# A gated attention block on one Trainium2 core: one more feature group by seven products, and one subtraction of the output pairs placed later

## The chip, the cores and the metric

The kernel runs on one core of one Trainium2 chip. The metric is the device time of one execution in microseconds (us); smaller is better. The kernel before takes 742.05 us, the median of 3 runs between 741.96 and 743.94.

## What is computed

```python
xn = layernorm(x)                                        # x: 2048 tokens x 640
q, k, v = split(xn @ wqkv)                               # 32 heads of 20
logits[s, w] = (q[s] . k[s - 2w]) * 20**-0.5             # w = 0..7; positions before the start are masked
s = (sum_w softmax(logits)[s, w] * v[s - 2w]) @ wo
g = silu(((xn @ w_gate) * (xn @ w_up)) @ w_down)         # 1536 features between
return x + s * g
```

All of it is fp32. TensorE multiplies in fp32r, so each operand is split into a high part (rounded to fp32r) and a low part (the rest), and each product is made of three: high by high, high by low, low by high (`ALL3`).

## The kernel before

The 2048 tokens are four chunks of 512, and the 1536 features are twelve feature groups of 128 (`f` = 0 to 11). `split` (L112) is the helper for the parts: ScalarE (ACT) copies the high part (L114), and the engine that is passed in subtracts it (L115), GpSimd (POOL) for nearly all weights.

**Two ways to make a feature group.** The straight way, `gate_up(f, ch)` (L636), is 15 matmuls of 512 columns for the gate and 15 for the up product of one chunk. The other way, `group(f, c0)` (L1296), makes gate and up of one feature group for two chunks together by Strassen's scheme (in its variant with seven products): seven products in the order j = 0, 5, 2, 1, 4, 3, 6, here called n0 to n6, with 6, 9, 6, 9, 6, 9 and 9 matmuls of 512 columns, 54 in place of 60. It needs sums of weight blocks (`w_add`: S1, S2, S3, d5, S4, all on POOL, L1281) and their high and low parts (`w_split`: G, S, R, U). The seven products pile up in three PSUM banks: A (tile name g), C (u) and B (q). After n0, n2, n3 and n4 ACT copies the bank out (`hold`, L1304) before a later product adds to it: n2 goes on A, which `hold` of n0 must have read, and n5 goes on C, which `hold` of n3 must have read. VectorE (DVE) and POOL put the copies together (L1307, L1310, L1313, L1317, L1320); L1310 and L1313 run on DVE for a group of chunks 2 and 3 with `f >= VEC`, else on POOL. L1320 releases bank A.

**Order of the work.** TensorE (PE) works through one list written out by hand. After a start with `f` = 0 and 1 and the first query/key/value blocks (`qkv`, L425) come `gate_up(1, 2)`, `gate_up(0, 3)`, `gate_up(1, 3)` (from L1169), then the `qkv` blocks of m = 1 to 4 (L1397 on), then a loop over f = 2 to 10 with `group(f, 2)` and `group(f, 0, 1)`, then `group(11)`, four straight products of `f` = 11 (L1363, L1372), ten tokens' worth of output pairs (`pair_product`, L1030), the rest of the output projection, and the down products (`product`, L895). In the loop, `two_places` puts the preparation of the weights of `f + 1` behind given products of the two groups: sums behind n5 and n6 of the first and n0 and n1 of the second, parts behind n2, n4, n5 and n6 of the second.

**Beside it.** The attention is a generator (L467) that `advance` lets go on by a credit after each piece of PE work; it is emitted in order, twelve units, each of DVE products and sums (L536, L543, L504), additions on POOL (L510), and one softmax with the exponent on ACT (L565) between two DVE steps (L563 and L570). Each engine works through its own queue in order, so what is emitted between two instructions sets what stands between them.

**Loads of weights.** `load_wf(f)` (L178, the transfer L180) brings 640 KB for one feature group into one of two buffers named wraw, which the sums of `w_add` share; the next load waits until the last reader of its buffer on POOL is done. The transfers are issued by SyncE (SP), which also has one queue in order.

**Output pairs.** For ten token tiles in pairs the output projection is made by seven products as well (`pair_product(p, j)`). `hi_pair` and `lo_pair` (L1021, DVE) make the parts of the next pair. After j = 0 to 2 ACT copies the bank into one buffer `o` (L1045); DVE adds from it at L1051, L1048 and L1053 (j = 5), and the next pair's first copy (L1045) must wait until L1053 has read the buffer. PE's next product on that bank waits for the copy.

## Time and profile before

| | |
|---|---|
| median of 3 runs | 742.05 us |
| profiled execution | 742.42 us |
| its span, first to last instruction | 740.0 us |
| mean granted TensorE clock | 0.999 |
| PE busy | 732.1 us, 99% |
| DVE busy | 625.0 us, 84% |
| POOL busy | 454.3 us, 61% |
| ACT busy | 302.5 us, 41% |

A line of the timeline has the start, the time, the engine, the line of the kernel, the operation, the tile written and the tiles read, the shape, and in square brackets how long the engine stood idle before it and on what. PEld is the load of PE's weights, which runs beside its matmuls. A line of the waits has the waiting instruction, what it waited for, the sum, the count and the longest. A line of the windows has the stretch, its length, and the busy time of PE, PEld, DVE, ACT and POOL. A line of the chain has start, duration and what it was; x15 is fifteen matmuls. A line of the groups has the count, the busy time, the mean in ns, and the idle time before.

### The profile page before, as it was taken

How to read it: one execution, taken by the hardware profiler on the slowest of the kernel's cores; microseconds unless marked ns; L12 is line 12 of the kernel's file. 1: busy time of each engine (PE TensorE's matmuls, PEld its weight loads, DVE VectorE, ACT ScalarE, POOL GpSimd, SP SyncE). 2: the span in 40 equal slices, each digit the busy share in tenths (PEclk: the TensorE clock that was granted, in tenths of full speed). 3: DMA queues.
4: the chain of work that ended last, by engine and by line, in shares of the span. 5: the costliest groups of instructions: out<-in, count | busy, mean ns of one | idle time of the engine just before them, and what ended most of it. 6: DMA issues, size and time to landing. Idle time of an engine off the chain costs nothing.

```text
span 740.0 us, 11087 instructions
## 1 busy us (share of the span) xinstructions
PE 732.1 (99%) x4048; PEld 667.8 (90%) x4048; DVE 625.0 (84%) x728; ACT 302.5 (41%) x578; POOL 454.3 (61%) x384
## 2 busy tenths in 40 slices
PE   8999999999999999999999999999999999999997
PEld 6989989988999998888888887888999999999997
DVE  7676998799787989899989999978998777777775
ACT  5668312423332333233233332335556664444442
POOL 6159919887688889798879979577559700000000
PEclk9999999999999999999999999999999999999999
DMA  9465582767364649452634443269558655555534
GB/s 325 166 203 173 216 276 88 241 220 241 93 183 144 232 152 362 119 186 60 205 100 127 153 128 101 83 180 243 149 160 235 223 208 193 192 193 192 193 107 142
DMA packets 103491, 132.96 MB, mean 180 GB/s; under 512 B 22696, under 2 KB 74404, under 8 KB 103438
## 3 DMA queue, kind: packets, MB, share of 16 engines
q1 hardware_dynamic: 86286, 114.25, 48.9%
q10 hardware_dynamic: 16000, 12.78, 5.3%
q0 software_dynamic: 1152, 5.24, 2.2%
q8 instruction: 31, 0.51, 0.3%
q14 instruction: 22, 0.18, 0.1%
HBM read 83.58 MB, written 47.81 MB: 178 GB/s over the span
## 4 chain that ended last, share of the span: by engine, by line
PE 94%; DMA 2%; DVE 1%; POOL 1%; issue 1%; ACT 1%; SPq 0%; ACTq 0%; DVEq 0%; POOLq 0%
PE g L1335 15%; PE q L433 10%; PE u L1335 10%; PE q L905 9%; PE u L433 8%; PE g L433 8%; PE u L905 6%; PE q L1335 5%; PE g L124 5%; PE u L124 5%; PE g L905 3%; PE e L905 3%; PE q L124 2%; PE e L433 1%; PE e L124 1%; PE q L1042 1%
## 5 line engine op out<-in xcount | busy, mean ns | idle before, releaser
L510 POOL TENSOR_TENSOR o<-o,t 128x960 f32<-128x960 f32 (+1 forms) x66 | 133.2, 2019 | 10.2 <-DVE t L504 9.4
L504 DVE TENSOR_TENSOR t<-e,kv 128x960 f32<-128x960 f32 (+1 forms) x96 | 99.6, 1038 | 16.4 <-POOL o L510 16.4
L536 DVE TENSOR_TENSOR t<-q,kv 128x1920 f32<-128x1920 f32 (+1 forms) x48 | 92.4, 1926 | 4.3 <-ACT s L447 2.9
L543 DVE TENSOR_REDUCE lg<-t 128x96 f32<-128x1920 f32 (+1 forms) x48 | 92.3, 1922 | 0.2
L433 PE MATMUL q<-s,xc 128*128 128x360 f32 (+1 forms) x450 | 83.1, 334 | 0.1
L115 POOL TENSOR_TENSOR s<-wraw,s 128x384 fp32r<-128x384 f32 (+6 forms) x57 | 69.6, 1235 | 19.3 <-ACT s L114 19.2
L1304 ACT ACTIVATE gh<-g 128x512 f32<-128x512 f32 x57 | 34.1, 599 | 113.5 <-PE g L1335 109.7
L433 PEld LDWEIGHTS q<-s,xc 128*128 128x128 f32 x450 | 74.9, 188 | 4.4 <-POOL s L115 0.6
L433 PE MATMUL u<-s,xc 128*128 128x360 f32 (+1 forms) x360 | 65.7, 334 | 0.0
L433 PEld LDWEIGHTS u<-s,xc 128*128 128x128 f32 x360 | 60.2, 188 | 2.3
L433 PE MATMUL g<-s,xc 128*128 128x360 f32 (+1 forms) x330 | 61.5, 337 | 0.0
L1335 PE MATMUL u<-xc,s 128*128 128x512 f32 x228 | 58.1, 390 | 0.0
L433 PEld LDWEIGHTS g<-s,xc 128*128 128x128 f32 x330 | 55.7, 188 | 2.6
L1335 PE MATMUL g<-s,s 128*128 128x512 f32 x228 | 57.9, 389 | 0.0
L905 PE MATMUL q<-xc,s 128*128 128x320 f32 x342 | 55.5, 309 | 0.0
L905 PEld LDWEIGHTS q<-xc,s 128*128 128x128 f32 x342 | 51.5, 188 | 0.0
L1335 PEld LDWEIGHTS u<-xc,s 128*128 128x128 f32 x228 | 42.8, 188 | 9.3 <-POOL s L115 0.4
L1335 PEld LDWEIGHTS g<-s,s 128*128 128x128 f32 x228 | 42.8, 188 | 8.8
L114 ACT ACTIVATE s<-wraw 128x384 fp32r<-128x384 f32 (+6 forms) x58 | 32.6, 581 | 29.8 <-PE g L1335 10.2
L1335 PE MATMUL g<-xc,s 128*128 128x512 f32 x171 | 42.0, 390 | 0.2 <-ACT gh L1304 0.2
L1335 PE MATMUL q<-xc,pk 128*128 128x512 f32 x171 | 41.8, 389 | 0.0
L510 POOL TENSOR_TENSOR o<-t 128x960 f32<-128x960 f32 (+1 forms) x11 | 22.1, 2011 | 28.9 <-DVE t L504 27.1
(364 smaller groups left out, 1563.6 us busy)
## 6 DMA issues: line engine op xcount, KB each, us to landing
h_scr<-gh SPq DMA_DIRECT2D x48, 256.0 KB, 2.6
wraw<-in_wgu SPq DMA_DIRECT2D x11, 640.0 KB, 4.6
kv<-qkv_scr SPq DMA_DIRECT2D x14, 480.0 KB, 5.7
t<-h_scr SPq DMA_DIRECT2D x8, 768.0 KB, 7.3
qkv_scr<-s ACTq DMA_DIRECT2D x17, 360.0 KB, 3.5
kv<-qkv_scr SPq DMA_DIRECT2D x14, 367.5 KB, 6.8
s_scr<-gh SPq DMA_DIRECT2D x16, 320.0 KB, 4.1
gh<-s_scr SPq DMA_DIRECT2D x16, 320.0 KB, 3.7
```

Source lines behind the costliest of these rows:

```text
L114: nc.scalar.activation(hi, raw, AF.Copy)
L115: eng.tensor_sub(lo, raw, hi.bitcast(F32))
L124: nc.tensor.matmul(acc, a, b, start=first and n == 0, stop=last and n == len(runs) - 1)
L433: nc.tensor.matmul(p, xT[(r * NE + i) // TPC][a][:, k, t0:t0 + P], wq[m][b][k], start=n == 0, stop=n == len(runs) - 1, skip_group_check=ac ...
L504: nc.vector.tensor_mul(t.rearrange("p (n d) -> p n d", d=DH), e[:, :, w].unsqueeze(2).to_broadcast([P, NE * nh, DH]), v)
L510: return NE * c * cost, lambda: eng.tensor_add(y, z, t)
L536: nc.vector.tensor_mul(t, q, k)
L543: nc.vector.tensor_reduce(out=lg[:, :, j:j + 2].rearrange("p n a -> p a n"), in_=t.rearrange("p a (n d) -> p a n d", d=DH), op=ALU.add, ax ...
L905: nc.tensor.matmul(p, y[:, i, k], wd_t[name][k][:, l], start=new and r == 0, stop=r == len(runs) - 1, skip_group_check=True)
L1042: nc.tensor.matmul(b, y, w, start=new and r == 0, stop=r == len(runs) - 1, skip_group_check=True)
L1304: nc.scalar.activation(kept[j], b["ACACABA"[j]], AF.Copy)
L1335: nc.tensor.matmul(y, w, x, start=j in (0, 1, 5) and r == 0, stop=r == len(runs) - 1, skip_group_check=True)
```

## The change

`gate_up(1, 2)` and `gate_up(1, 3)` go; feature group 1 of chunks 2 and 3 is made by `group(1, 2)` after the `qkv` blocks and ahead of `group(2, 2)`. Its weights, which the start has already loaded and split in another form for chunks 0 and 1, are loaded again. All that was prepared for `f` = 2 during the `qkv` blocks is now prepared for `f` = 1, and the weights of `f` = 2 are prepared within `group(1, 2)` itself, behind n2 to n6. `VEC` is 1, so that L1310 and L1313 of the new group are on DVE. Apart from that, `lo_pair(p + 1, 1)` goes behind `pair_product(p, 5)`.

```diff
-VEC = 2
+VEC = 1
     split_wq(1, nc.gpsimd)
-    gate_up(1, 2)
     gate_up(0, 3)
-    gate_up(1, 3)
-    F_TWO = 2
+    F_TWO = 1
     def first_parts():
         for name in ("S1", "S2", "S3", "d5", "S4"):
-            w_add(2, name)
+            w_add(1, name)
             yield
-        w_split(2, "S")
+        w_split(1, "S")
             if (m, r, i) == (last - 1, 1, 6):
-                load_wf(2)
+                load_wf(1)
             elif m == last and n == NT - 3:
-                w_split(2, "G")
+                w_split(1, "G")
     step(100)
-    w_split(2, "R")
-    w_sum.pop(2)
-    load_wf(3)
+    w_split(1, "R")
+    w_sum.pop(1)
+    load_wf(2)
-    for f in range(2, f1):
+    for f in range(1, f1):
         places.clear()
+        if f == 1:
+            places.update({(0, 2): splits("G"), (0, 3): sums("S1", "S2"), (0, 4): sums("S3", "d5", "S4"),
+                           (0, 5): splits("S"), (0, 6): splits("R", "U")})
+            group(1, 2)
+            continue
         places.update(two_places)
-        if f == F_TWO:
+        if f == 2:
             for n in range(3):
                 places[0, n] = lambda f, n=n: load_late(n)
         group(f, 2)
@@
         wd_splits()
         if more:
             lo_pair(p + 1, 2)
+        pair_product(p, 5)
+        if more:
             lo_pair(p + 1, 1)
-        pair_product(p, 5)
```

The diff moves the lines of `group` up by two: `hold` is L1304 before and L1302 after, `w_add`'s sum L1281 and L1279, the copies' additions L1307 to L1320 are L1305 to L1318.

**ACT at the first group.** The rows from the last parts of the weights ahead of the first group to its third and fourth `hold`. Before, where the first group is `group(2, 2)` (its banks are g_2641 and u_2642):

```order
L114 ACTIVATE s_2636<-wraw_2292 128x384
L114 ACTIVATE s_2636<-wraw_2226 128x384
L1304 ACTIVATE gh_2651<-g_2641 128x512
L565 ACTIVATE e_70<-lg_2449 128x256
L494 ACTIVATE q_2_69<-q_2543 128x640
L1304 ACTIVATE gh_2682<-g_2641 128x512
L1304 ACTIVATE gh_2696<-u_2642 128x512
```

Of the change, where it is `group(1, 2)` (g_2542 and u_2543); wraw_2540 is the weights of `f` = 2, wraw_2594 their sums:

```order
L114 ACTIVATE s_2537<-wraw_2190 128x384
L114 ACTIVATE s_2537<-wraw_2129 128x384
L1302 ACTIVATE gh_2552<-g_2542 128x512
L1302 ACTIVATE gh_2572<-g_2542 128x512
L114 ACTIVATE pk_2488<-wraw_2540 128x640
L1302 ACTIVATE gh_2592<-u_2543 128x512
L1302 ACTIVATE gh_2606<-g_2542 128x512
L114 ACTIVATE s_2353<-wraw_2594 128x768
L114 ACTIVATE s_2537<-wraw_2594 128x384
L114 ACTIVATE s_2537<-wraw_2540 128x384
L1302 ACTIVATE gh_2650<-g_2642 128x512
```

The high part of G of `f` = 2 now stands between the second and the third `hold` of the group, and three more high parts stand ahead of the first `hold` of the next group.

**POOL at the same place**, of the change: from the low part of G of `f` = 1 (wraw_2129) to that of U of `f` = 2. The third row from the top is an addition of the attention; the fourth is the low part of R of `f` = 1, the last reader of the buffer into which `f` = 2 is loaded.

```order
L115 TENSOR_TENSOR pk_2488<-wraw_2129,pk_2488 128x640
L510 TENSOR_TENSOR o_2469<-t_941 128x640
L510 TENSOR_TENSOR o_2469<-o_2469,t_941 128x640
L115 TENSOR_TENSOR s_2537<-wraw_2190,s_2537 128x384
L115 TENSOR_TENSOR s_2537<-wraw_2129,s_2537 128x384
L510 TENSOR_TENSOR o_2469<-o_2469,t_941 128x640
L115 TENSOR_TENSOR pk_2488<-wraw_2540,pk_2488 128x640
L1279 TENSOR_TENSOR wraw_2594<-wraw_2540 128x256
L1279 TENSOR_TENSOR wraw_2594<-wraw_2594,wraw_2540 128x256
L510 TENSOR_TENSOR o_2469<-o_2469,t_941 128x640
L1279 TENSOR_TENSOR wraw_2594<-wraw_2540 128x256
L1279 TENSOR_TENSOR wraw_2594<-wraw_2540 128x128
```

Before, the like rows of R and U (s_2636) were followed by loads and by the attention's next unit; no sum of the next feature group stood within the first group's first five products.

**ACT at the exponent of the tenth unit**, in `group(6, 2)` (bank g_3403 before, g_3413 after). Before:

```order
L1304 ACTIVATE gh_3411<-g_3403 128x512
L1304 ACTIVATE gh_3442<-g_3403 128x512
L1304 ACTIVATE gh_3454<-u_3404 128x512
L565 ACTIVATE e_70<-lg_3180 128x384
L494 ACTIVATE q_2_69<-q_3294 128x960
```

and of the change:

```order
L1302 ACTIVATE gh_3421<-g_3413 128x512
L1302 ACTIVATE gh_3447<-g_3413 128x512
L1302 ACTIVATE gh_3459<-u_3414 128x512
L1302 ACTIVATE gh_3469<-g_3413 128x512
L565 ACTIVATE e_70<-lg_3214 128x384
```

The exponent has moved from behind the third `hold` of this group (n3) to behind the fourth (n4).

**DVE in the first output pair.** The rows at the sum L1053, before:

```order
L1048 TENSOR_TENSOR gh_4784<-o_4544,u_4756 128x320
L1051 TENSOR_TENSOR gh_4796<-o_4544,q_1_68 128x320
L1021 TENSOR_TENSOR s_4773<-t_4549,s_4773 128x768
L1021 TENSOR_TENSOR xc_4542<-s_4727,xc_4542 128x640
L1053 TENSOR_TENSOR gh_4784<-o_4544,g_4806 128x320
```

and of the change:

```order
L1048 TENSOR_TENSOR gh_4797<-o_4557,u_4769 128x320
L1051 TENSOR_TENSOR gh_4809<-o_4557,q_1_68 128x320
L1021 TENSOR_TENSOR s_4786<-t_4562,s_4786 128x768
L1053 TENSOR_TENSOR gh_4797<-o_4557,g_4818 128x320
L1021 TENSOR_TENSOR xc_4555<-s_4740,xc_4555 128x640
```

L1053 has moved ahead of one low part of 128x640.

## The prediction

> **What bounds the kernel now.** I read the page's busy line first, then the chain that ended last, then the waits of PE and of its weight load, and then the timeline at the places that the change touches. The busy line:
>
> ```profile
> PE 732.1 (99%) x4048; PEld 667.8 (90%) x4048; DVE 625.0 (84%) x728; ACT 302.5 (41%) x578; POOL 454.3 (61%) x384
> ```
>
> PE is busy for 732.1 of 740.0 us. So the end is set by how many matmuls there are and by the few places where PE waits. The chain gives their pitch: fifteen of 512 columns in 3.40 us are 0.227 us each, fifteen of 360 columns in 2.40 us are 0.160 us each.
>
> ```profile
> 84.71 3.40 PE g L124 x15
> 105.11 2.40 PE q L433 x15
> 273.67 2.04 PE q L1335 x9
> 285.91 2.04 PE q L1335 x9
> ```
>
> The last two rows are the same product of two groups in a row, 12.24 us apart, that is 54 x 0.227: within a group before, PE waits for nothing. The waits of the weight load say where it does:
>
> ```profile
> PEld e L1042 <- ACT o L1045: 1.0, 2, 0.6
> PEld q L1042 <- ACT o L1045: 0.9, 2, 0.5
> PEld g L124 <- DVE gh L1320: 0.3, 1, 0.3
> ```
>
> Four waits of the output pairs (L1042) make about 1.9 us, and one, small, stands where the last feature group's straight products need a bank from DVE.
>
> **The change, part by part.** *Matmuls.* Two `gate_up` of 30 go and one group of 54 comes: 6 matmuls fewer, 6 x 0.227 = 1.36 us less for PE. What moves is larger: 13.60 us leave the place at 84.71 to 105.11, so all `qkv` blocks begin 13.6 us earlier, and 12.24 us come back behind them.
>
> *The first `qkv` block of m = 1.* Its weights' low parts are made by POOL:
>
> ```profile
> 89.13 4.39 POOL L115 TENSOR_TENSOR s<-wraw,s 128x1080 fp32r<-128x1080 f32 x3
> ```
>
> They end at 93.52. Before, the block begins at 105.11. Now it begins at 84.71 + 6.80 = 91.51, and its tenth matmul, the first that likely needs the last of these parts, at 91.51 + 9 x 0.160 = 92.95. That is a wait of about 0.6 us (0 if the parts come sooner, 2.0 if the block's first matmul needs them all).
>
> *The load of f = 2.* This is the largest term. The rows of before at its first group, the nearest to the new one:
>
> ```profile
> 259.78 1.57 POOL L510 TENSOR_TENSOR o<-t 128x640 f32<-128x640 f32 x1
> 262.29 1.56 POOL L510 TENSOR_TENSOR o<-o,t 128x640 f32<-128x640 f32 x1 [0.94 <-DVE t L504]
> ...
> 268.62 0.74 ACT L114 ACTIVATE pk<-wraw 128x640 fp32r<-128x640 f32 x1 [0.60 <-ACT s L447]
> 269.43 1.57 POOL L115 TENSOR_TENSOR pk<-wraw,pk 128x640 fp32r<-128x640 f32 x1 [1.26 <-ACT pk L114]
> ...
> 272.15 1.52 PE L1335 MATMUL g<-xc,pk 128*128 128x512 f32 x6
> ...
> 275.77 2.02 POOL L115 TENSOR_TENSOR s<-wraw,s 128x384 fp32r<-128x384 f32 x2
> ...
> 276.84 0.35 SPq L180 DMA_DIRECT2D wraw<-in_wgu  x1
> ...
> 279.15 0.60 ACT L1304 ACTIVATE gh<-u 128x512 f32<-128x512 f32 x1 [1.44 <-PE u L1335]
> ...
> 280.31 2.20 PE L1335 MATMUL u<-xc,s 128*128 128x512 f32 x9
> ...
> 282.90 0.73 POOL L1281 TENSOR_TENSOR wraw<-wraw 128x256 f32<-128x256 f32 x1
> ```
>
> The parts R and U are the two POOL rows at 275.77; the next feature group is loaded right behind R, at 276.84, and its sums, the first that read it, begin at 282.90, 6 us later. From issue to landing such a load takes:
>
> ```profile
> DMA to landing us min/median/max: 4.2/4.5/5.4
> ```
>
> In the change the first reader is ACT, which makes the high part of G behind the second `hold` of the same group, so there are no 6 us. Its time, step by step. The group begins at 272.15 - 13.6 + 0.6 = 259.15. The attention does not move: DVE is emitted at the same credit per `qkv` block, 13.6 us of credit are gone with the `gate_up`, and its waits on POOL stay. G's high part of f = 1 ends at 268.62 + 0.74 - 13.0 = 256.4, its low part at 258.0; then two additions of the attention stand ahead of R in POOL's queue, 4.07 us for the two in the rows at 259.78 and 262.29, to 262.05; R to 263.1; landing at 263.1 + 4.5 = 267.6. The high part of G takes 0.74, to 268.35, and behind it in ACT's queue stands the `hold` of n3, 0.60, to 268.95. PE wants to begin n5, which goes on that bank, at 280.31 - 272.15 = 8.16 us into the group: 267.31. **First stall: 1.7 us.**
>
> Behind that, POOL has a whole set of weights to make before the third product of the next group. The groups of before, from 272 to 500 us:
>
> ```profile
> L115 POOL TENSOR_TENSOR s<-wraw,s 128x384 fp32r<-128x384 f32 x19 | 21.8, 1152 | 0.0
> L115 POOL TENSOR_TENSOR s<-wraw,s 128x768 fp32r<-128x768 f32 x9 | 16.7, 1851 | 5.8 <-ACT s L114 5.8
> L1281 POOL TENSOR_TENSOR wraw<-wraw 128x256 f32<-128x256 f32 x18 | 15.7, 874 | 17.6 <-DMA wraw<-in_wgu 17.6
> L114 ACT ACTIVATE s<-wraw 128x768 fp32r<-128x768 f32 x9 | 7.5, 838 | 0.0
> ```
>
> From 268.35: low part of G 1.57, S1 and S2 0.74 each (0.73 in the row at 282.90), an addition 1.57, S3, d5 and S4 some 1.9 (estimated from that row and the mean of 0.87), S's high part 0.84: 275.75; its low part 1.85, an addition 1.57, R and U 2.02: 281.2. The next group begins at 259.15 + 12.24 + 1.7 = 273.1. Its first `hold` stands on ACT behind the high parts of S, R and U, about 276.7 to 277.3, and n2 wants that bank at 276.5: 0.9 us. The last matmul of n3 reads U's low part and is ready at 280.4: 0.8 us. **Together 3.4 us** (1.5 with the shortest landing and one addition fewer ahead of R, 5.9 with the longest and one more). After that the old rhythm holds, in which sums follow loads by more than a group.
>
> *DVE, which keeps this.* A late PE would be free to lose its lead again, but DVE cannot make it good. It is nearly full, and its softmax waits for an exponent that stands on ACT behind a `hold`, so behind PE:
>
> ```profile
> 412.00:449.00 37.00, 37.00 (x164) 30.63 (x164) 35.98 (x33) 13.45 (x23) 30.53 (x24) 1.00 0.31 93
> ```
>
> ```profile
> 377.37 0.60 ACT L1304 ACTIVATE gh<-u 128x512 f32<-128x512 f32 x1 [1.74 <-PE u L1335]
> 377.86 0.49 ACT L565 ACTIVATE e<-lg 128x384 f32<-128x384 f32 x1
> ...
> 378.38 0.56 DVE L570 TENSOR_REDUCE sm<-e 128x48 f32<-128x384 f32 x1 [2.79 <-ACT e L565]
> ```
>
> DVE waits 2.79 us for this exponent, behind n3 of `group(6, 2)`. By the order of the change it stands behind n4, a product of six matmuls or 1.36 us later. PE is there -1.36 + 0.6 + 3.4 us late, so DVE resumes 1.36 - 1.36 + 0.6 + 3.4 = 4.0 us late. From there it is full up to the flush of the attention, which holds back the load of the output weights and a run of DVE work whose end releases PE's bank:
>
> ```profile
> 483.49 0.36 SPq L584 DMA_DIRECT2D o_scr<-o  x1
> ...
> 486.30 2.35 SPq L697 DMA_DIRECT2D t<-in_wo  x4
> ...
> 491.15 2.18 DVE L945 TENSOR_TENSOR kv<-t 128x640 f32<-128x640 f32 x1 [4.69 <-DMA t<-in_wo]
> ```
>
> ```profile
> 508.19 0.68 DVE L1320 TENSOR_TENSOR gh<-gh,g 128x512 f32<-128x512 f32 x1
> ...
> 508.93 3.09 PEld L124 LDWEIGHTS g<-xc,s 128*128 128x128 f32 x14 [0.28 <-DVE gh L1320]
> ```
>
> PE already waits here for DVE. So it leaves this place by DVE's 4.0 us late, and the 1.36 us are gone: they only lengthen this wait. L1310 and L1313 of the new group on DVE (0.7 us each in the quiet, 2.7 us at most beside POOL) come ahead of DVE's wait at 378.38, which covers them; uncovered they would cost 1.4 to 5.4 us.
>
> *The output pairs.* In 520 to 559 us:
>
> ```profile
> 520.00:559.00 39.00, 38.18 (x255) 37.13 (x254) 37.38 (x59) 23.53 (x53) 21.40 (x19) 1.00 0.59 164
> ```
>
> ```profile
> 526.95 1.50 DVE L1021 TENSOR_TENSOR xc<-s,xc 128x640 fp32r<-128x640 f32 x1
> ...
> 528.38 0.47 DVE L1053 TENSOR_TENSOR gh<-o,g 128x320 f32<-128x320 f32 x1
> ...
> 528.97 0.44 ACT L1045 ACTIVATE o<-e 128x320 f32<-128x320 f32 x1 [3.83 <-DVE gh L1053]
> ...
> 529.46 0.88 PEld L1042 LDWEIGHTS e<-xc,s 128*128 128x128 f32 x6 [0.58 <-ACT o L1045]
> ```
>
> The chain of this wait stands in four rows: low part, sum L1053, copy L1045, PE. With L1053 ahead of the low part it runs 528.38 - 526.95 = 1.43 us sooner. DVE is full through the stage, so the lead is won once, not four times: 1.4 us of the 1.9, with 0.4 (what one pair waits) and 1.9 as the ends. The low part, 0.47 later, is needed in the next pair only.
>
> **The sum.** The profiled execution took 742.42, 0.37 over the median; the differences are the same from either, and I count from 742.05: + 4.0 (DVE's lateness, which holds the 0.6 and the 3.4 and swallows the 1.36) - 1.4 = 744.65, rounded **744.7 us**. With the ends of the stall and of the pairs it is 742.3 to 748.1.
>
> **The rivals.** *It does what it says.* If f = 2 is in place when ACT reaches the high part of G, PE never stalls. The point: the load must land 1.7 us sooner than I have it, by 265.9, which it does if the attention's additions fall behind R instead of ahead of it. And the end must not be bound by DVE. Then 742.05 - 1.36 - 1.4 = 739.3. For it speaks that 4.5 us of landing and 8.16 us of group leave room if R is ready when the group begins; against it POOL's order.
>
> *The load is in time, but DVE sets the end.* Then 0.6 from the first block passes through the exponent and the pairs' gain remains: 742.05 + 0.6 - 1.4 = 741.2.
>
> *The stall is there, but DVE catches up* by 508 us, for instance because POOL's additions are less late: 742.05 - 1.36 + 0.6 + 3.4 - 1.4 = 743.3. Against it stands the full DVE row of 412 to 449.
>
> *A slower clock behind the stall.* The rows of all stretches show a granted clock of 1.00, also that of the start, where PE is idle a third of the first 4 us:
>
> ```profile
> 0.00:4.00 4.00, 2.65 (x4) 1.51 (x5) 0.99 (x3) 1.28 (x1) 3.08 (x22) 1.00 0.51 139
> ```
>
> If one gap made the clock fall to half for as long as the gap lasted, 3.4 us of matmuls would take 3.4 us more; half of that, since DVE sets the end anyway, gives 746.4. The Trainium skill ("TensorE: Matmul & The Clock Gate", What's actually happening) has such a rule, half rate after an idle window of about 3.4 us; my stalls are three, the longest 1.7, and the row of the start shows no half rate, so it has little weight.
>
> **Chances.** The forecast 0.54, of which 0.43 end more than 0.3% slower; the slower clock 0.05; DVE catches up 0.12; load in time but DVE bound 0.12; it does what it says 0.17. A measurement of this kernel tells about 0.3% (2.2 us) from no change. Faster by more than that: 0.17 of the last and 0.01 of the one before it, 0.18. Slower: 0.43 + 0.05 = 0.48. Within: 0.34. The range that leaves out 2 in 10 or less reaches from 739.2, so that most of the faster case is in it, to 747.3; the likeliest case's own is 742.3 to 748.1.
>
> **What would show it.** In the new group, PE's n5 waits for ACT's `hold` at L1302, and that `hold` stands behind a high part L114 of G that waited for wraw from in_wgu: right. If PE runs n0 to n6 in 12.24 us, the largest term is wrong. PE waits for a low part of L115 near 93 us by 0.6. The exponents near 380 us are about 4 us later, and the wait of L124 on DVE's L1318 near 512 us is well over 0.3 us. The waits of L1042 on L1045 shrink from 1.9 to 0.5. I am wrong if the load of f = 2 is issued before the group begins, or if DVE reaches its flush at 483.5 as before.

## The result, and the profile after

The changed kernel takes 751.02 us (median of 4 runs, 750.42 to 751.89), the kernel before 743.00 us beside it (4 runs, 741.96 to 744.81): ratio 1.011, 95% interval 1.0087 to 1.0133. It is slower by 8 us, and lies 3.7 us above the range. The profiled execution took 750.42 us with a span of 748.6 us, 8.6 us more than the 740.0 of before.

The busy line of the page, and the waits of PE:

```profile
PE 736.7 (98%) x4042; PEld 671.5 (90%) x4042; DVE 619.9 (83%) x731; ACT 306.8 (41%) x584; POOL 465.1 (62%) x393
```

```profile
PE g L1333 <- POOL pk L115: 2.3, 1, 2.3
PE u L1333 <- POOL s L115: 1.9, 2, 1.1
...
PE u L1333 <- ACT gh L1302: 1.3, 1, 1.3
PE q L433 <- POOL s L115: 0.5, 1, 0.5
```

PE has 6 matmuls fewer, as it should, and is yet *busy* 4.6 us longer. So the loss has two kinds: waits, which stand in the second list, and matmuls that take longer, which no list of waits shows. For these one has to look at the pitch. The timeline of PE at the first `qkv` blocks of m = 1 (L433):

```profile
91.31 1.69 PE L433 MATMUL q<-s,xc 128*128 128x360 f32 x9
93.48 1.26 PE L433 MATMUL q<-s,xc 128*128 128x360 f32 x6 [0.47 <-POOL s L115]
94.58 2.63 PE L433 MATMUL g<-s,xc 128*128 128x360 f32 x15
97.05 2.63 PE L433 MATMUL u<-s,xc 128*128 128x360 f32 x15
```

The wait stands at the tenth matmul, as forecast: 93.48 - 91.31 is 2.17 us for nine matmuls that need 1.44, so 0.7 us were lost. But the next block begins 2.47 us after the one before (94.58 to 97.05), where it was 2.40 us before the change. 2.47/15 is 164.4 ns for a matmul of 360 columns in place of 160.0. This goes on to the end of the `qkv` stage; about 710 matmuls of this size follow, so 710 x 4.4 ns = **3.1 us**. The granted clock is 1.00 all along:

```profile
96.00:258.00 162.00, 162.00 (x911) 155.04 (x910) 132.49 (x119) 49.43 (x97) 125.93 (x85) 1.00 0.58 183
```

`group(1, 2)` therefore begins at 262.53 and not at 259.15. The forecast stall in it, of ACT, SP and PE:

```profile
262.53 1.54 PE L1333 MATMUL g<-xc,pk 128*128 128x512 f32 x6
...
265.86 1.99 POOL L115 TENSOR_TENSOR s<-wraw,s 128x384 fp32r<-128x384 f32 x2
...
266.90 0.35 SPq L180 DMA_DIRECT2D wraw<-in_wgu  x1
...
270.94 0.74 ACT L114 ACTIVATE pk<-wraw 128x640 fp32r<-128x640 f32 x1 [2.82 <-DMA wraw<-in_wgu]
...
271.58 0.58 ACT L1302 ACTIVATE gh<-u 128x512 f32<-128x512 f32 x1
...
272.21 2.37 PE L1333 MATMUL u<-xc,s 128*128 128x512 f32 x9 [1.33 <-ACT gh L1302]
```

n5 waits for the `hold`, the `hold` stands behind the high part of G, and that waited for the load, which SP issued right behind R. By start to start of PE's matmuls the three pieces (270.5, 279.6, 283.3 us) cost 1.49 + 0.27 + 0.91 = 2.7 us. Then comes what was not foreseen, 20 us later, inside `group(2, 0, 1)`. The chain that ended last at this place:

```profile
285.87 1.58 POOL s L1189 x3
...
289.08 10.14 DMA o_scr<-o
...
299.36 1.57 POOL o L510
```

The attention's finished unit is stored from its one buffer `o` (L584), issued at 289.08, and needs 10.14 us to land. POOL's next addition into `o` stands at the head of POOL's queue and waits for it, idle for 7.7 us; the low parts and the last three sums of f = 3 stand behind it. PE and POOL there, in the timeline:

```profile
299.36 1.57 POOL L510 TENSOR_TENSOR o<-t 128x640 f32<-128x640 f32 x1 [7.70 <-DMA o_scr<-o]
...
304.21 1.56 POOL L115 TENSOR_TENSOR pk<-wraw,pk 128x640 fp32r<-128x640 f32 x1
...
305.82 0.74 PE L1333 MATMUL g<-xc,pk 128*128 128x512 f32 x2 [2.33 <-POOL pk L115]
...
306.40 3.50 PE L1333 MATMUL q<-xc,pk 128*128 128x512 f32 x9
```

Nine matmuls take 3.50 us behind this gap, not 2.04 to 2.2: eight of them run at 427 ns in place of 227. The windows show it in the granted clock (third from the end of a row, behind the busy times of the five engines) of 300 to 312:

```profile
284.00:300.00 16.00, 15.61 (x69) 12.94 (x70) 10.58 (x15) 5.04 (x9) 8.23 (x11) 1.00 1.01 332
300.00:312.00 12.00, 9.68 (x36) 7.50 (x35) 10.39 (x11) 2.75 (x5) 12.00 (x11) 0.86 0.51 161
```

This place costs 2.5 (the gap) + 1.6 (the clock) + 1.3 (U's low part, at 313) = **5.4 us**. The first row also shows why the store is slow: from 284 to 300 the DMA engines are full (share 1.01, 332 GB/s). These are mainly the late transfers (L1189 and L1193, 3.4 MB, issued by POOL between 285.8 and 290.1), ahead of the store or beside it. Before, the same transfers ran at 277.7, *behind* the store of 275.86. How long each store took to land, before and after:

```profile
DMA to landing us min/median/max: 2.9/2.9/2.9
```

```profile
DMA to landing us min/median/max: 10.1/10.1/10.1
```

At the end of the program the output pairs went nearly as forecast. The wait of the last group's straight product for DVE did not: forecast was well over 0.3 us, and it is 0.27, as before. Both places:

```profile
519.59 3.28 PEld L124 LDWEIGHTS g<-xc,s 128*128 128x128 f32 x15 [0.27 <-DVE gh L1318]
```

```profile
520.00:559.00 39.00, 39.00 (x242) 37.01 (x241) 35.01 (x53) 22.29 (x45) 25.02 (x19) 1.00 0.69 192
```

PE is busy for all of the 39 us; of the four waits of the pairs 0.2 us are left of 1.9. The ledger, from PE's starts: - 1.4 (six matmuls) + 0.8 (first block) + 3.1 (pitch) + 2.7 (first group) + 5.4 (second) - 2.3 (pairs, and two small waits at 376 and 453 us that are gone) = + 8.3 of the 8.6; the rest is pieces of 0.5 us and less.

### The profile page after: what moved, and what is told of

The parts are those of the page before. It is cut to its first block, busy times and chain, and to the rows that moved or that the text cites. A ratio compares the mean times of both kernels' runs of the same rounds, so it can differ in the third digit from the quotient of the medians.

```text
span 748.6 us, 11088 instructions
## 1 busy us (share of the span) xinstructions
PE 736.7 (98%) x4042; PEld 671.5 (90%) x4042; DVE 619.9 (83%) x731; ACT 306.8 (41%) x584; POOL 465.1 (62%) x393
## 4 chain that ended last, share of the span: by engine, by line
PE 85%; POOL 9%; DMA 2%; issue 1%; DVE 1%; ACT 1%; POOLq 0%; DVEq 0%; ACTq 0%
PE g L1333 14%; PE q L433 9%; PE u L1333 9%; PE q L905 8%; PE u L433 7%; PE g L433 7%; PE u L905 6%; PE q L1333 4%; PE g L905 3%; PE e L905 3%; PE q L124 2%; PE g L124 2%; POOL kv L602 2%; PE u L124 2%; POOL o L510 2%; PE q L1042 2%
## 5 line engine op out<-in xcount | busy, mean ns | idle before, releaser
L543 DVE TENSOR_REDUCE lg<-t 128x96 f32<-128x1920 f32 (+1 forms) x48 | 92.3, 1923 | 0.2
L115 POOL TENSOR_TENSOR s<-wraw,s 128x384 fp32r<-128x384 f32 (+6 forms) x60 | 72.9, 1227 | 21.5 <-ACT s L114 20.6
L433 PE MATMUL q<-s,xc 128*128 128x360 f32 (+1 forms) x450 | 84.3, 337 | 0.6 <-POOL s L115 0.5
L1302 ACT ACTIVATE gh<-g 128x512 f32<-128x512 f32 x60 | 35.9, 599 | 117.9 <-PE g L1333 111.6
L433 PEld LDWEIGHTS q<-s,xc 128*128 128x128 f32 x450 | 75.9, 188 | 5.0 <-POOL s L115 1.2
L433 PE MATMUL u<-s,xc 128*128 128x360 f32 (+1 forms) x360 | 66.9, 337 | 0.0
L1333 PE MATMUL u<-xc,s 128*128 128x512 f32 x240 | 61.6, 391 | 3.2 <-POOL s L115 1.9
L433 PEld LDWEIGHTS u<-s,xc 128*128 128x128 f32 x360 | 61.3, 188 | 2.2
L433 PE MATMUL g<-s,xc 128*128 128x360 f32 (+1 forms) x330 | 62.5, 340 | 0.0
L1333 PE MATMUL g<-s,s 128*128 128x512 f32 x240 | 61.5, 392 | 0.1
L433 PEld LDWEIGHTS g<-s,xc 128*128 128x128 f32 x330 | 56.7, 188 | 2.6
L1333 PEld LDWEIGHTS u<-xc,s 128*128 128x128 f32 x240 | 45.0, 188 | 13.7 <-POOL s L115 2.7
L1333 PEld LDWEIGHTS g<-s,s 128*128 128x128 f32 x240 | 45.4, 190 | 10.0 <-ACT gh L1302 0.5
L114 ACT ACTIVATE s<-wraw 128x384 fp32r<-128x384 f32 (+6 forms) x61 | 34.5, 584 | 39.8 <-PE g L1333 10.2
L1333 PE MATMUL q<-xc,pk 128*128 128x512 f32 x180 | 45.3, 398 | 0.0
L1333 PE MATMUL g<-xc,s 128*128 128x512 f32 x180 | 44.0, 389 | 0.0
```

The source lines that it names most:

```text
L114: nc.scalar.activation(hi, raw, AF.Copy)
L115: eng.tensor_sub(lo, raw, hi.bitcast(F32))
L433: nc.tensor.matmul(p, xT[(r * NE + i) // TPC][a][:, k, t0:t0 + P], wq[m][b][k], start=n == 0, stop=n == len(runs) - 1, skip_group_check=ac ...
L543: nc.vector.tensor_reduce(out=lg[:, :, j:j + 2].rearrange("p n a -> p a n"), in_=t.rearrange("p a (n d) -> p a n d", d=DH), op=ALU.add, ax ...
L1302: nc.scalar.activation(kept[j], b["ACACABA"[j]], AF.Copy)
L1333: nc.tensor.matmul(y, w, x, start=j in (0, 1, 5) and r == 0, stop=r == len(runs) - 1, skip_group_check=True)
```

## The experiments

The theory after this: the 8 us are two things that the forecast lacks, a slower pitch that begins with the 0.7 us wait, and a store that met the late transfers; the first group's stall is as forecast, and the pairs' gain too. Rivals: the pitch belongs to what runs beside the blocks; POOL's amount of work, and not the store, makes the stall at 303.

### 1. Only the subtraction moved

```diff
             lo_pair(p + 1, 2)
-            lo_pair(p + 1, 1)
         pair_product(p, 5)
+        if more:
+            lo_pair(p + 1, 1)
```

> The kernel before with only the one subtraction of the output pairs placed later, no other edit. Theory (the sum L1053 held up the copy that PE waits for): the four waits of L1042 on L1045, 1.9 us in the kernel before and 0.25 in the changed one, go to about 0.25 us, so the span is 1.4 to 1.7 us shorter, about 741.4 us. Rival (in the changed kernel the waits went because PE came late to this stage and DVE had caught up): the waits stay at 1 us or more and the time moves by less than 0.7 us.

740.49 us (12 runs) against 742.88: 0.9969 (0.9952 to 0.9985), the ratio to the kernel before and its 95% interval, as behind the time of every run below. No wait of PE on L1045 is left; the span is 738.1, 1.9 less. The copy's rows at the first pair:

```profile
526.95 0.47 DVE L1053 TENSOR_TENSOR gh<-o,g 128x320 f32<-128x320 f32 x1
527.35 1.10 DVE L1021 TENSOR_TENSOR xc<-s,xc 128x640 fp32r<-128x640 f32 x1
...
527.54 0.44 ACT L1045 ACTIVATE o<-e 128x320 f32<-128x320 f32 x1 [2.40 <-DVE gh L1053]
```

The copy comes at 527.54 in place of 528.97, 1.43 us sooner, the very number of the forecast. This half of the change is a gain, and it is the fastest kernel of all that ran.

### 2. The weights of m = 1 split earlier

```diff
     low_parts()
+    split_wq(1, nc.gpsimd)
     early_high(1)
...
-    split_wq(1, nc.gpsimd)
```

> The changed kernel, with the low parts of the query/key/value weights of m = 1 ahead of eight other POOL operations, so that PE does not wait at 92.6 us. Theory (the wait of 0.7 us put PE's matmuls of 360 columns from a pitch of 160 ns to one of 164.4 ns, which lasts until groups begin): no wait, pitch 160 ns up to the first group, which begins 0.8 + 3.1 = 3.9 us sooner; the stalls behind it, which hang on POOL's chain, take part of this back, so the total is 1 to 4 us shorter than the changed kernel's 751.0, 747 to 750. Rival (the pitch of 164 ns comes from what runs beside PE in the changed kernel, DVE, POOL or transfers): only the wait goes, the pitch stays at 164 ns and the first group begins 0.8 us sooner.

755.4 us, 1.0161 (1.014 to 1.0181). The wait at 93 is gone and the pitch is 160 ns up to 106 us. Then PE waits 3.8 us for a copy on ACT, whose queue stood behind a high part that waited for weights; their load left SP at 102.72 in place of 97.76, since SP's stores ahead of it waited for POOL. From there the pitch is 164.4. So the slower pitch began at another wait, 13 us later, and not at the first block: this speaks for the theory. As a remedy it failed.

### 3. The late transfers spread out

```diff
-            for n in range(3):
-                places[0, n] = lambda f, n=n: load_late(n)
+            places[0, 0] = lambda f: load_late(0)
+            places[0, 3] = lambda f: load_late(1)
+            places[0, 5] = lambda f: (load_late(2), w_add(f + 1, "S1"))
```

> The changed kernel, with the late transfers from t_scr and e_scr in group(2, 2) spread: two behind n0 as now, one behind n3, two behind n5. Theory (the store of the attention's unit at 289 us lands only after 10.1 us because 3.4 MB of these transfers stand ahead of it; POOL waits 7.7 us for its buffer, the weights of f = 3 come late, and PE waits 2.3 us at 303 us, loses 1.6 us to half the clock and waits 1.1 us at 314): the store lands in under 6 us, POOL's wait goes to under 3 us, and the total is 4 to 5.3 us shorter than 751.0, 745.7 to 747. Rival (POOL is late anyway since the weights of f = 2 were late): PE still waits over 2 us in group(2, 0), and less than 2 us are won.

751.14 us, 1.0111 (1.0094 to 1.0129), no gain. POOL's queue put the three issues at 285.97, 288.60 and 289.17, still around the store, which now left at 288.70. It held POOL for 6.9 us, and its landing was as slow, 9.9 us.

What was expected fell: an issue that is written behind a later product doesn't come later when POOL lags behind PE.

### 4. R earlier, so that f = 2 is loaded sooner

```diff
                 w_split(1, "G")
+                w_split(1, "R")
+                w_sum.pop(1)
+                load_wf(2)
...
-    w_split(1, "R")
-    w_sum.pop(1)
-    load_wf(2)
```

> The changed kernel, with the parts of R of f = 1 and the load of f = 2 two qkv blocks earlier, right behind the parts of G. Theory (the first stall is the high part of G of f = 2 waiting on ACT for the load, with a hold behind it): the load is issued 4 us or more sooner, PE's waits at 270.5 (1.5 us), 280 (0.3) and 283 us (0.9) go, 2.5 to 3 us, and the total falls by 2.5 us or more, to 748.5 or less. Rival (POOL is full from there on, and what is not waited for here is waited for in group(2, 0)): these waits go, but the wait at 303 us grows by as much, and the total moves by less than 1 us.

749.07 us, 1.0078 (1.0057 to 1.0099). The load leaves SP at 264.13, 0.9 us behind the group's start (263.21) where it was 4.4, and n5 does not wait:

```profile
269.03 0.74 ACT L114 ACTIVATE pk<-wraw 128x640 fp32r<-128x640 f32 x1 [0.21 <-DMA wraw<-in_wgu]
...
271.42 2.20 PE L1333 MATMUL u<-xc,s 128*128 128x512 f32 x9
```

The first piece of the stall hangs on when R is done, as forecast. The stall at 303 stays, and the clock with it.

### 5. One low part of m = 1 on DVE

```diff
-    split_wq(1, nc.gpsimd)
+    split_wq(1, nc.gpsimd, (0, 4))
+    split_wq(1, nc.vector, (4, KD))
```

> The changed kernel, with the fifth low part of the query/key/value weights of m = 1 made by DVE in place of POOL, nothing else moved. Theory (the wait of 0.7 us at 92.6 us sets PE's matmuls of 360 columns to a pitch of 164.4 ns for the whole qkv stage): no wait there, pitch 160.0 ns from 91 us to the first group, which begins 3.5 to 4 us sooner than in the changed kernel (at 258.5 to 259 us). Since the load of f = 2 is bound by POOL, part of it is then waited for at the first group's n5: total 1 to 4 us under the changed kernel's. Rival (the pitch comes from what runs beside PE): the pitch stays 164.4 ns and the group begins 0.8 us sooner.

751.45 us, 1.0099 (1.0068 to 1.0129). The wait shrank to 0.23 us and nothing was won: the pitch is still 164.4, and the stall at 303 grew from 2.5 to 3.6 us. So a third of the wait brought the whole of the slower pitch.

### 6. The late transfers ahead of the store

```diff
-            places.update({(0, 2): splits("G"), (0, 3): sums("S1", "S2"), (0, 4): sums("S3", "d5", "S4"),
+            places.update({(0, 0): lambda f: load_late(0), (0, 1): lambda f: load_late(1),
+                           (0, 2): lambda f: (load_late(2), w_split(f + 1, "G")), (0, 3): sums("S1", "S2"), (0, 4): sums("S3", "d5", "S4"),
                            (0, 5): splits("S"), (0, 6): splits("R", "U")})
...
-        if f == 2:
-            for n in range(3):
-                places[0, n] = lambda f, n=n: load_late(n)
```

> The changed kernel, with all the late transfers from t_scr and e_scr behind n0 to n2 of group(1, 2) in place of group(2, 2), so 12 us sooner and ahead of the attention's store at 289 us. Theory (the store lands late because it shares the DMA engines with transfers issued just ahead of it; so POOL waits 7 us and PE 3.4 us with 1.6 us of half clock behind): the store lands in under 6 us, PE's waits at 303 to 314 us go, 4 to 5.5 us; but the load of f = 2 at 267 us now shares the engines with them and lands 1 to 5 us later, which the first stall shows. Net 0 to 4 us shorter. Rival (POOL's lateness at 300 us comes from the late weights of f = 2): PE waits at 303 us as before.

745.47 us (10 runs, 744.25 to 746.16), 1.0021 (1.0002 to 1.0041): 5.5 us better than the change by the medians. The store between the two groups, and the windows at the two places:

```profile
DMA to landing us min/median/max: 2.8/2.8/2.8
```

```profile
266.00:278.00 12.00, 9.40 (x40) 7.14 (x39) 10.02 (x10) 2.76 (x5) 11.91 (x15) 1.00 1.04 336
300.00:312.00 12.00, 12.00 (x53) 9.64 (x52) 10.61 (x14) 3.12 (x7) 12.00 (x10) 1.00 0.30 90
```

The stalls at 303 to 314 are gone, with POOL just as full there (12.00 of 12.00): the store was the cause and not POOL's amount of work. In turn the load of f = 2 now lands beside the transfers (share 1.04), and the first stall grew from 1.5 to 2.6 us, without a fall of the clock. In this profiled run the wait at 93 us (0.75) was *not* followed by the slower pitch: fifteen took 2.40 us. So a wait can draw it and need not. It also means that the 5.5 us are not the store's alone. Between the two profiled executions (750.42 and 744.25) the pitch makes 3.1 us; by PE's starts the stretch from 300 us on won 5.4 and the two groups ahead of it lost 1.8. Which pitch the other nine executions had is not known.

### 7 and 8. The remedies together

Run 7 has the edits of runs 4 and 6, run 8 those of 4, 5 and 6.

> The changed kernel with two edits: the parts of R of f = 1 and the load of f = 2 two qkv blocks earlier, and the late transfers behind n0 to n2 of group(1, 2). Theory (two causes, each with its own wait: the late load of f = 2, and the store behind the late transfers): PE waits less than 1.5 us in all between 262 and 330 us, and no stretch has half the clock, against 8.4 us of waits and slow clock in the changed kernel: total 743.0 to 745.5. Rival (POOL's work beside the groups of f = 1 and 2 is too much, whatever the order): over 3 us of waits stay there, total over 746.

> The changed kernel with three edits: the fifth low part of m = 1 on DVE, the load of f = 2 two qkv blocks earlier, the late transfers behind n0 to n2 of group(1, 2). If all of the lost time is in the three places (the first qkv block with the pitch behind it 3.9 us, the load of f = 2, the store), this has the 1.36 us of fewer matmuls and the 1.6 us of the output pairs left: 739 to 741, under the kernel before. If the qkv stage's 3.9 us only move the start of the first group while POOL's chain sets its pace, waits of 2 to 4 us come up there, and the total is 742 to 745.

746.38 us (10 runs, one at 743.55, the others from 746.0), 1.0029 (1.001 to 1.0048), and 745.86 us, 1.003 (1.0013 to 1.0046). Neither beats run 6. Both have one stall left, in run 7 this one:

```profile
281.27 2.80 PE L1333 MATMUL g<-s,s 128*128 128x512 f32 x6 [2.58 <-ACT gh L1302]
```

It is the first `hold` of `group(2, 2)`, which stands on ACT behind three high parts that wait for POOL's sums. In run 8 POOL is without a gap from 267 to 288 us. What PE wins ahead of this place it waits for here.

### 9. Thirty matmuls of 512 columns among the blocks

The changed kernel with thirty more matmuls of 512 columns behind the eighth block of m = 1, whose result nobody reads.

```diff
             qkv(m, r, i)
+            if (m, n) == (1, 7):
+                y = pt([P, CH], "g", 2)
+                for k in range(30):
+                    nc.tensor.matmul(y, xT[3][0][:, 0, :P], xT[3][0][:, 0, :], start=k == 0, stop=k == 29)
```

> The changed kernel with thirty extra matmuls of 512 columns, whose result nothing reads, after the eighth qkv block of m = 1 (6.8 us of PE added). Theory: the pitch of PE's matmuls of 360 columns is a state that a wait of PE can set to 164.4 ns and that a long row of matmuls of 512 columns sets back to 160 ns. So, if the eight blocks after the wait at 93 us run at 164.4 ns, those behind the thirty matmuls run at 160.0 ns up to the first group, 590 x 4.4 ns = 2.6 us less than without them. Rival (the pitch follows what runs beside PE in the qkv stage): the pitch behind them is 164.4 ns again.

756.23 us in one run. PE's timeline around them:

```profile
109.67 2.63 PE L433 MATMUL g<-s,xc 128*128 128x360 f32 x15
112.13 6.98 PE L1412 MATMUL g<-xc 128*128 128x512 f32 x30
118.95 2.56 PE L433 MATMUL u<-s,xc 128*128 128x360 f32 x15
121.35 2.56 PE L433 MATMUL q<-s,xc 128*128 128x360 f32 x15
```

Ahead of them a block takes 2.46 us from start to start (109.67 to 112.13), behind them 2.40 (118.95 to 121.35). So the slower pitch is a state, and a row of 512-column matmuls ends it. The 240 matmuls of 480 columns that lie within the stage do not: in the change the pitch is 164.4 ns ahead of them and behind them. The time did not follow: the first group's stall grew to 2.7 us with a fallen clock, since POOL did not move.

### 10 and 16. The kernel before, again

> The kernel before, unchanged. Its times fall in two heaps, about 742 and 745 us. If the heaps are the two pitches, this run, where it is near 745, shows a pitch of 164.4 ns in the qkv stage; where it is near 742, it shows 160.0 ns as the profile of before does. If it is near 745 at a pitch of 160 ns, the heaps have another cause.

> The kernel before, unchanged, for one more profile. Theory (its times near 745, 3 us above the others, are the slower pitch of about 700 qkv matmuls, drawn by chance): if the run is near 745, fifteen 360-column matmuls take 2.47 us in it; if it is near 742, 2.40. Rival: a run near 745 with 2.40 us for fifteen.

742.16 and 741.99 us, both at 2.40 us for fifteen. The executions of the kernel before near 745 us were not met with a profile; whether they are the slower pitch is open.

### 11, 12 and 15. Less for POOL

Run 11 is run 8 with the late transfers issued by SP and the parts of S, R and U of f = 2 made behind the first `hold` of `group(2, 2)`, the low one of S on DVE. Run 12 has two low parts of m = 1 on DVE and S back on POOL, in the first group. Run 15 is run 12 with a third one on DVE, and the low parts of R and U too. Two places of run 11's edit:

```diff
-        nc.gpsimd.dma_start(tt[0][n], t_scr[:, 3 * n:3 * n + 3])
+        if n == 0:
+            nc.gpsimd.dma_start(tt[0][n], t_scr[:, 3 * n:3 * n + 3])
+        else:
+            nc.sync.dma_start(tt[0][n].bitcast(F32), t_scr[:, 3 * n:3 * n + 3])
...
+        if f == 2:
+            places[0, 0] = lambda f: (w_split(f, "S", eng=nc.vector), w_split(f, "R", "U"), w_sum.pop(f), wf_raw.pop(f))
```

> The kernel with the three edits (fifth low part of m = 1 on DVE, load of f = 2 two qkv blocks earlier, late transfers ahead of the attention's store) and three more: the late transfers are issued by SP in place of POOL (2.7 us of POOL's queue), S, R and U of f = 2 are split behind the first hold of group(2, 2), and the low part of S of f = 2 is on DVE. Theory (with the transfers out of the way, what is left at 278 us is POOL's chain of sums for f = 2, with ACT's hold behind the high parts that wait for it: 2.7 us and about 2 us of half clock): PE waits less than 1 us between 262 and 330 us, no half clock, total 738 to 742. Rival (POOL's chain is too long for one group whatever is taken off): PE still waits over 2 us for a part of S or u5, total 743 or more.

744.34 us, 1.0015 (0.9996 to 1.0035). One stall of 2.1 us is left, on S's low part, which DVE made slowly beside POOL:

```profile
277.12 1.86 DVE L1318 TENSOR_TENSOR gh<-gh,gh 128x512 f32<-128x512 f32 x1
278.90 2.29 DVE L115 TENSOR_TENSOR s<-wraw,s 128x768 fp32r<-128x768 f32 x1
```

> As the kernel with the late transfers on SP, with two edits: the fourth low part of m = 1 is on DVE too, so that PE does not wait at 93 us at all, and S of f = 2 is split by ACT and POOL behind n5 of group(1, 2) again, its low part ahead of two additions of the attention. Theory (a wait of any length lets the pitch of 360 columns fall to 164.4 ns, no wait leaves it at 160; and what is left at 279 us is the low part of S behind two additions or behind DVE's own work): pitch 160.0 ns in the whole qkv stage, the first group begins 3 us sooner than at 164.4, PE waits less than 1.5 us between 258 and 330 us, total 738.5 to 741, under the kernel before and at or under the kernel with the output pairs' edit alone (740.5). Rival (POOL's chain sets the end of group(1, 2)): the 3 us come up as a wait for a part of G, S or u5 there, total 742 to 744.

745.77 us, 1.0035 (1.0019 to 1.005). A wait of 0.1 us at 92.3 us was left, and the pitch is 164.4 behind it. U's low part, behind two additions of the attention, made a stall of 2.8 us with a fallen clock.

> The kernel of the twelfth run with two more low-part makers moved off POOL: the third low part of m = 1 on DVE too, and the low parts of R and U of f = 2 on DVE at n0 of group(2,2). Theory (a wait near 92 us sets the pitch, and U's low part behind two additions of the attention makes the only stall left): no wait, pitch 2.40 us, no stall over 1 us at group(2,2), so 740 to 742 us, faster than before by 0.1 to 0.3%. Rival (POOL's sums, not U's low part, set the end of the stall, and DVE is full): a stall of 1.5 to 3 us remains near 280 us, 743 to 745.5.

745.22 us (12 runs, 741.73 to 748.93), 1.0016 (0.9997 to 1.0035). The median is the rival's. The profiled execution was among the short ones (742.07): no wait at 92, 2.40 us for fifteen, and three stalls in place of one, of 1.5, 1.1 and 1.0 us. So removing one wait at the second group uncovers the next. Why most executions are 3 us longer than the profiled one is open.

### 13 and 14. The wait alone, taken away and put in

Run 13, the changed kernel:

```diff
-    split_wq(1, nc.gpsimd)
+    split_wq(1, nc.gpsimd, (0, 2))
+    split_wq(1, nc.vector, (2, KD))
```

> The changed kernel with the last three of the five low parts of m = 1 on DVE, in place of POOL, so that they are ready long before 92 us. Theory (the wait at 92.6 us, however short, sets the slower pitch of the qkv matmuls): no wait of PE between 88 and 96 us, fifteen 360-column matmuls in 2.40 us to the end of the qkv blocks, the first group 3.9 us sooner; of that little is kept, since POOL's sums for f = 2 and the store between 289 and 299 do not move, 749 to 751. Rival (the pitch comes from what runs beside the blocks, whose order the change altered, and not from the wait): no wait, but still 2.47 us for fifteen, 750 to 752.

Run 14, the kernel before:

```diff
-    split_wq(1, nc.gpsimd)
+    split_wq(1, nc.gpsimd, (0, 4))
     gate_up(1, 2)
     gate_up(0, 3)
     gate_up(1, 3)
+    split_wq(1, nc.vector, (4, KD))
```

> The kernel before with one edit: the fifth low part of m = 1 is made on DVE behind the three straight products, so that PE waits about 2 us for it in the first qkv block of m = 1, near 106 us. Nothing of the change is in it. Theory (a wait there sets the slower pitch): 2 us of wait, then 2.47 us for fifteen 360-column matmuls for the rest of the stage, 3.1 us; 1 to 2 us more if the clock halves; 747 to 749 us. Rival (the slower pitch belongs to the change's order and not to a wait): the wait, then 2.40 us for fifteen, 744.5 to 745.5 us.

PE's timeline of run 13, then that of run 14:

```profile
91.49 2.56 PE L433 MATMUL q<-s,xc 128*128 128x360 f32 x15
93.89 2.56 PE L433 MATMUL g<-s,xc 128*128 128x360 f32 x15
```

```profile
104.93 1.60 PE L433 MATMUL q<-s,xc 128*128 128x360 f32 x9
108.31 1.26 PE L433 MATMUL q<-s,xc 128*128 128x360 f32 x6 [1.77 <-DVE s L115]
109.41 2.63 PE L433 MATMUL g<-s,xc 128*128 128x360 f32 x15
```

Without the wait the changed kernel runs its blocks 2.40 us apart up to the first group. With a wait the kernel before, which has nothing of the change, runs them 2.46 to 2.47 us apart (164.4 ns on average, to the end of the stage). So the pitch follows a wait and not the change's order, though by run 6 not every wait brings it. Run 14 takes 747.88 us, 1.0062 (1.004 to 1.0084): 5.0 us for a wait of 1.9 and its 3.1. Run 13 takes 749.33, 1.0076 (1.0056 to 1.0097), 1.7 us better than the change: of the 3.8 us by which its first group begins sooner (258.69) more than half is waited for again, since the load, POOL and the store stand where they stood. Its stalls are 2.7 and 3.6 us, both with half rate behind them; the window of the second has a clock of 0.72:

```profile
300.00:312.00 12.00, 8.56 (x26) 6.49 (x26) 10.90 (x12) 2.50 (x5) 12.00 (x12) 0.72 0.39 131
```

## Why the prediction was right in direction and wrong in size

Two steps of the sum failed: the pitch of the blocks behind the first wait, and the second group, which was put at nothing. A third, DVE's lateness, did not come. That the kernel became slower at all, as forecast, is luck: without the two terms that were missed the ledger reads - 1.4 + 0.8 + 2.7 - 2.3 = - 0.2, no change. The forecast without DVE's lateness was 743.3, which is no change that could be told from the noise either.

- *Six matmuls fewer*: right, 4048 to 4042. That the 1.36 us are swallowed by DVE was wrong, see below.
- *The first `qkv` block*: right as a wait (0.6 forecast, 0.7 measured, at the tenth matmul). Wrong was what it left out: "Now it begins at 84.71 + 6.80 = 91.51" moved all blocks with their old 0.160 us. The wait put them at 164.4 ns, 3.1 us. Runs 13 and 14 show that it is the wait. The chain of the kernel before holds both pitches in its own start, behind short waits and behind matmuls of 512 columns, so one figure for all blocks was not safe:

```profile
18.95 2.47 PE q L433 x15
...
34.59 2.40 PE q L433 x15
```

- *The load of f = 2*: right, in mechanism and size. 2.7 us for 3.4: 1.5 and 1.2 us for the two parts, where 1.7 (1.64 by its own numbers) and 1.7 were forecast. Run 4 takes the first away by R alone.
- *"After that the old rhythm holds, in which sums follow loads by more than a group"*: this step failed, 5.4 us. I followed PE's, ACT's and POOL's queues through the first two groups and stopped there. I looked at the late transfers as three issues on POOL and not as 3.4 MB that something else has to pass: the group shifts them from behind a store to ahead of it, and the store's buffer holds back POOL. Run 6 shows it (landing 2.8 us, the stalls gone), run 3 that spreading them does not help.
- *DVE, which keeps this*: not borne out. The exponent did move behind n4:

```profile
390.46 0.49 ACT L565 ACTIVATE e<-lg 128x384 f32<-128x384 f32 x1
390.98 0.56 DVE L570 TENSOR_REDUCE sm<-e 128x48 f32<-128x384 f32 x1 [1.45 <-ACT e L565]
```

  DVE resumes 12.6 us later than before (390.98 for 378.38). But its flush store comes 10.9 us later:

```profile
494.35 0.36 SPq L584 DMA_DIRECT2D o_scr<-o  x1
```

  So DVE won back 1.7 us in 103 us, although it also stood idle for 3.8 us ahead of four additions L1305, which lie multiples of 12.24 us apart, a group's length (the profile names no releaser): it had time to spare. "DVE catches up" was the better case here, and a busy share of 36 of 37 us was no proof that nothing can be regained. The sentence "PE already waits here for DVE" misread its row as well. The 0.28 us (0.27 in the change) are idle time of the weight load; from the product ahead to this one PE takes 3.42 us for fifteen matmuls in both kernels, against 3.40 without a wait.
- *The output pairs*: right. 1.4 forecast, 1.6 in the ledger, 1.9 of span in run 1.
- *A slower clock*: the rival at 0.05 did come, but as a small part (1.6 us) and behind a gap that was not forecast. The Trainium skill ("TensorE: Matmul & The Clock Gate", What's actually happening) has the half rate after an idle window of about 3.4 us. Here gaps of 2.0 to 2.8 us already brought it (run 4 and run 9 at 2.0, the change at 2.5), and not every one did, so the measurement decides against 3.4 us as the bound for a gap. The prediction's row of 0 to 4 us could not speak against a slower clock: its column shows 1.00, but the records of the clock begin at 4.5 us before and at 6.7 us in the change, and the four matmuls q<-lg (L229) that begin at 4.07 us take 1.26 us before and 1.92 in the change.

The two failed terms, 3.1 and 5.4, are 8.5 us. The 4.0 forecast for DVE stood in for the stall, and the 1.36 was kept after all; with both terms the sum - 1.4 + 0.7 + 3.1 + 3.4 + 5.4 - 1.4 is 9.8. The first group was 0.7 cheaper than that and the pairs, with the two small waits, 0.9: 8.2, against 8.0 by the medians.

## What to carry to other kernels

When a change shifts a stage in time, list every bulk transfer and every store near it and see whether their order turns round: here a store of 320 KB that landed in 3 us ahead of 3.4 MB took 10 us among them, and a single-buffered tile passes that on to a whole queue. Where an engine makes all weights for the next step, what is won ahead of its chain is waited for at its end, so measure the halves of a change apart: the half here that only moved one subtraction gained 0.3%, and the other half lost more than 1%. And of a short wait ask what it does to the work behind it, not only how long it is.

## What the runs showed of the hardware

**Two pitches of one matmul.** Rows of 360-column matmuls ran at 160.0 or at 164.4 ns with a granted clock of 1.00. In the `qkv` stage the slower pitch began at waits of PE of 0.1 us (run 12), 0.2 (runs 5, 8 and 11), 0.7 (the change and runs 3, 4, 7 and 9), 1.9 (run 14) and 3.8 (run 2). Once it did not follow one (run 6), and no profile without a wait there had it. A block at 42 us, in which all 18 profiles have a wait of about 0.16 us, runs at the slower pitch behind that wait in 17 of them and at 160.0 in run 4. Rows of 512 columns ended it (30 matmuls in run 9). Matmuls of 480 columns took 216.7 ns on average in both states. What in the chip keeps this state the runs do not show.

**Half rate behind short gaps.** Of 17 gaps of PE between 2.0 and 4.0 us in these runs, 13 were followed by matmuls at a lower rate, mostly five to eight of 512 columns at 427 ns (a clock of 0.86 in the window of 12 us; twelve and 0.72 behind the 3.6 us of run 13). The other four, of 2.1 (run 11), 2.4 (run 2), 2.6 (run 6) and 3.6 us (run 5), were not. None of the seven of 1.4 to 1.9 us was. The length of a gap does not decide alone; where it falls does. While matmuls run, the half rate lasts 3.41 us (twice that once in run 2 and once in run 13), and in each profile its beginnings lie on a grid of 3.41 us. The rows below are, of the change, a stretch of this grid with the gap in it and the half rate behind it, then, of run 5, the two stretches into which its 3.6 us fall:

```profile
303.64:307.05 3.41, 1.23 (x5) 1.04 (x6) 3.41 (x5) 0.53 (x2) 3.41 (x3) 1.00 0.40 91
307.05:310.47 3.42, 3.42 (x9) 2.66 (x9) 3.42 (x5) 0.15 (x1) 3.42 (x4) 0.50 0.00 0
```

```profile
301.68:305.09 3.41, 1.61 (x8) 1.00 (x6) 3.22 (x4) 1.78 (x3) 3.41 (x5) 1.00 0.98 345
305.09:308.51 3.42, 1.81 (x8) 1.51 (x9) 3.42 (x4) 0.60 (x1) 3.42 (x4) 1.00 0.06 16
```

Behind the first 9 us, and by the starts of its matmuls, PE stood idle for 2.1 us or more in each of the 13 stretches ahead of a fall, and for less than 2.0 us in every other one. So a gap of 2.0 us that lies within one stretch can halve the clock, and one of 3.6 us that lies across a border need not.

**DVE beside POOL.** The addition gh<-gh,gh of 128x512, which takes 0.68 us in the change at 293.46 (L1311), while POOL waits for the store, took 1.86 in run 11 (L1318 there), while POOL worked. That POOL is the reason is not shown by a run of its own.
